# A transformer block, forward and backward, on one core: three groups of DMA issues moved in SyncE's and GpSimd's queues

## The chip, the core and the metric

The kernel runs on one core of a Trainium2 chip. The metric is the device time of one execution in microseconds (us). The time before is 819.68 us, the median of 3 runs (819.25 to 820.12).

## The reference

One layer with its gradients: S = 2048 rows, D = 640, 32 heads of 20, F = 1728, all bf16. The function returned is the layer's output and, for a given grad_out, the gradients of x, wqkv, wo, w1, w3 and w2.

```python
def _A_ref(x, wqkv, wo):                       # linear attention
    q, k, v = split_heads(x @ wqkv)
    phi = lambda t: jnp.where(t > 0, t + 1, jnp.exp(t)) + 1e-6
    pq, pk = phi(q), phi(k)
    kv = jnp.einsum("bhsd,bhse->bhde", pk, v)
    z = jnp.einsum("bhsd->bhd", pk)
    num = jnp.einsum("bhqd,bhde->bhqe", pq, kv)
    den = jnp.einsum("bhqd,bhd->bhq", pq, z)[..., None] + 1e-6
    return merge_heads(num / den) @ wo
def _B_ref(x, w1, w3, w2):                     # gated MLP
    return (jax.nn.silu(x @ w1) * (x @ w3)) @ w2
h = x + _A_ref(_layernorm(x), wqkv, wo)
h2 = h + _B_ref(_layernorm(h), w1, w3, w2)
```

(split_heads and merge_heads stand for the reference's reshapes and transposes.)

## The kernel before, in words

The rows are cut into 16 tiles of 128 (ST = 16), D into 5 blocks of 128 (DT = 5), F into 14 (FT = 14). Work is issued in the order in which the Python code runs: every engine has its own queue, executes it in order, and waits on semaphores where its data comes from another engine or from a DMA. Nothing is reordered afterwards. DMAs written `dma` and `dmaT` (a DMA that transposes) are issued by SyncE (SP), those written `dmaG` by GpSimd (POOL), some by ScalarE (ACT). A DMA issue that waits holds back all later issues of its queue.

The stages on TensorE, with the trace's times:

- 0 to 60 us: LayerNorm 1 of x, its transposed form pqT, and k for all tiles (L266 to L280). Beside it M = pk^T x is summed block by block (`m_part`, L425, L430): M's block m is a [128, 640] piece, copied out by ScalarE in `m_end` (L433, L437) and turned into mT by a DMA (L442).
- 60 to 85 us, the stretch that the change touches (L586 to L642, then the list in `run` at L950): the remaining blocks of M, q for tiles 5 to 15 (`q_tile`, `q_late`), kv = wv^T mT block by block (`kvT_block`, L444 to L451), and Wp, the product of kv and wo (`f2_wT`, L703). Each of Wp's five pieces is turned by a DMA of SyncE (L711). For each tile t, r = pq / den is made by `r_prod` (GpSimd, L367), `r_red`, `r_inv` and `r_scale` (VectorE, L374 to L381; together `r_row`), and turned into pqT by `r_T` (a DMA of SyncE, L385); `r_head` is `r_row` and `r_T`.
- 85 to 97 us: `f2_at` (L651 to L671) multiplies r's tiles 0 to 5 with Wp (L659; for some halves an identity product with x first, L657), adds x, and takes the statistics of LayerNorm 2. `f2_hn` (L750) writes the normalized tile hn. Tiles 0 and 1 are turned into hnT by a DMA of SyncE (L766 in `f2_ht`), tiles 2 and 3 by TensorE (L770) and a ScalarE copy (L771). hn is also stored to memory for the backward pass (L758).
- from 97.6 us: the MLP, four chunks of 512 rows (`mlp`, L788). Each step multiplies w1, w3 and w2^T with a chunk (`mm5_to`, L393 to L396). Then the gradients, to the end.

Loads that the change speaks of:

- `w13` (L500, L501) is a list of seven loads of w1 and w3: rows 0-255, 256-511 and 512-639 of each, and a last small one for w1's padding. `w13[4:]` is the last block of 128 rows of w1 and of w3 and the small one.
- `load_x(0, 4)` (L186) loads rows of x again into x_sb, where the normalized x was; the normalized x is what M's blocks multiply (L431).
- `load_w2T(a, b)` (L456) loads and turns rows a to b of w2.
- `f2_m_out` (L716) stores M's block 4, `r_store(5, 6)` (L735) stores r's tile 5, both from GpSimd.
- `f2_rest` (L673) finishes the held halves of tiles 4 and 5.

In `f2_hn` hn's tile 0 is not stored at once: the line reads `for n in ((), (0, 1))[t] if t < 2 else (t,)`, so that tiles 0 and 1 are stored behind the turn of tile 1.

Of the kernel before, what the change touches and what calls it, by code (L numbers as in the profile page):

```python
# [9 lines left out]
P = 128  # L10
# [13 lines left out]
W, SC, TPC = 512, 4, 4  # L24
# [31 lines left out]
def kernel(  # L56
# [20 lines left out]
    dma, dmaT, dmaG = SY.dma_start, SY.dma_start_transpose, G.dma_start  # L77

    def rows(ap):
        return ap.rearrange("(t p) d -> p t d", p=P)  # L80
# [22 lines left out]
    r_v, pk_v, xn_v, hn_v, m_v, pq_v = rows(r_d), rows(pk_d), rows(xn_d), rows(hn_d), rows(m_d), rows(pq_d)  # L103
# [82 lines left out]
    def load_x(a, b):  # L186
        dma(out=x_sb[:, a:b, :], in_=xS[:, a:b, :])
# [40 lines left out]
    def load_w13(c0, c1):  # L228
        def go1():
            dma(out=w1[:, c0:c1, 0:F], in_=rows(B_w1)[:, c0:c1, :])  # L230

        def go3(c0=c0, c1=c1):
            dma(out=w3[:, c0:c1, :], in_=rows(B_w3)[:, c0:c1, 0:F - FL])
        return [go1, go3]
# [39 lines left out]
    def p1_mm(t, n0, between=None, halves=None):  # L274
        acc = p1_acc() if halves is None else None
        for j in range(2):
            p1_half(acc[:, j, 0:HD] if halves is None else halves[j][:, 0:HD], t, n0 + j * HD)
            if j == 0 and between is not None:
                between()
        return acc  # L280
# [9 lines left out]
    def phi(acc, dst, t, parts=None):  # L290

        mq, rq = parts or phi_tiles()
        if parts is None:
            kw = dict(scale=ln1.rs[:, t:t + 1]) if t < RAW else {}
            A.activation(two(mq[:]), acc[:, :, 0:HD], AF.Exp, **kw)
            A.activation(two(rq[:]), acc[:, :, 0:HD], AF.Relu, **kw)

        def rest():
            V.tensor_scalar(out=mq[:], in0=mq[:], scalar1=1.0, scalar2=1e-6, op0=ALU.min, op1=ALU.add)
            V.tensor_tensor(out=dst, in0=mq[:], in1=rq[:], op=ALU.add)  # L300
        held.append(rest)
# [9 lines left out]
    def q_home(t):  # L311
        if t < 4 or 8 <= t < 10:
            pqs[t] = pq6[:, t if t < 4 else t - 4, :]
        elif t < 8:
            pqs[t] = pf.tile([P, D], BF16, name="pql", bufs=4)[:]
        else:
            pqs[t] = pkx[0][:, DT + t - 10, :]
# [3 lines left out]
    def q_tile(t):  # L321
        q_home(t)
        phi(p1_mm(t, 0), pqs[t], t)
# [7 lines left out]
    def z_diag(m):  # L331
        dz[m] = hx[:, 10, m * P:(m + 1) * P]
        V.tensor_scalar(out=dz[m], in0=ident[:], scalar1=Z[:, m:m + 1], scalar2=None, op0=ALU.mult)
# [25 lines left out]
    def r_prod(t):  # L359
        for j in range(2):  # L360
            js = slice(j * HD, (j + 1) * HD)
            if t < 8:
                pr[t, j] = (p1.tile([P, HD], F32, name="pr", bufs=2) if t % 2 else
                            pf.tile([P, HD], F32, name="pr", tag="h2", bufs=2))[:]
            else:
                pr[t, j] = ps.tile([P, 512], F32, name="prp", tag="at", bufs=2)[:, 0:HD]
            (G if t < 8 else V).tensor_tensor(out=pr[t, j], in0=pqs[t][:, js], in1=Zb[:, js], op=ALU.mult)  # L367
# [4 lines left out]
    def r_red(t, js=(0, 1)):  # L372
        for j in js:
            V.reduce_sum(out=rden[:, t, j * 16:(j + 1) * 16], in_=heads(pr.pop((t, j))), axis=AX.X)  # L374

    def r_inv(t):
        V.tensor_scalar(out=rden[:, t, :], in0=rden[:, t, :], scalar1=1e-6, scalar2=None, op0=ALU.add)
        V.reciprocal(out=rden[:, t, :], in_=rden[:, t, :])

    def r_scale(t):  # L380
        V.tensor_tensor(out=heads(pqs[t]), in0=heads(pqs[t]),  # L381
                        in1=rden[:, t, :].unsqueeze(2).to_broadcast([P, H, DH]), op=ALU.mult)

    def r_T(t):
        dmaT(out=pqT[:, :, t * P:(t + 1) * P], in_=pqs[t])  # L385
# [39 lines left out]
    def m_part(m, tiles, js=(0, 1)):  # L425
        if m not in macc:
            macc[m] = [ps.tile([P, 512], F32, name="macc", tag=("m", "tr")[m % 2], bufs=2) for _ in range(2)]
        for t, j in [(t, j) for t in tiles for j in js]:
            n = HD + (m < 2) * j
            T.matmul(macc[m][j][:, 0:n], lhsT=pk_all[:, t, m * P:(m + 1) * P],  # L430
                     rhs=x_ext[:, t, j * HD:j * HD + n], start=(t == 0), stop=(t == ST - 1))  # L431

    def m_end(m, js=(0, 1)):  # L433
        mb = mbs[:, m % 4, :]
        acc = macc[m]
        for j in js:
            A.copy(out=mb[:, j * HD:(j + 1) * HD], in_=acc[j][:, 0:HD])  # L437
        if m < 2:
            A.copy(out=Z[:, m:m + 1], in_=acc[1][:, HD:HD + 1])
            z_diag(m)  # L440
        if m < DT - 1:
            dmaT(out=mT[:, :, m * P:(m + 1) * P], in_=mb)  # L442

    def kvT_block(m, acc):  # L444

        a, b = M_H[m]
        n = (b - a) * DH
        for c in range(DT):
            T.matmul(acc[:, 0:n], lhsT=wqkv[:, c, 2 * D + m * P:2 * D + (m + 1) * P],
                     rhs=mT[:, c, a * DH:b * DH], start=(c == 0), stop=(c == DT - 1))  # L450
        masked(bd, acc[:, 0:n], m)  # L451
# [48 lines left out]
    w13 = [go for c0, c1 in ((0, 2), (2, 4), (4, 5)) for go in load_w13(c0, c1)]  # L500
    w13 += [lambda: dma(out=w1[:, :, F:FP], in_=rows(B_w3)[:, :, F - FL:F])]  # L501

    def load_wo():
        dma(out=wo[:], in_=A_wo.rearrange("(c p) n -> p c n", p=P))
# [69 lines left out]
    def big():  # L574
        return ps.tile([P, 2, 512], F32, name="bigx", tag="big", bufs=2)[:, 0]

    def r_row(t):
        r_red(t)
        r_inv(t)
        r_scale(t)  # L580

    def r_head(t):
        r_row(t)
        r_T(t)
# [16 lines left out]
    m_part(2, range(10, ST))  # L601
    m_end(2)
    load_wo()
    for go in w13[4:]:
        go()
    dmaG(out=m_v[:, 0, :], in_=mbs[:, 0, :])
    r_head(0)
    r_prod(2)
# [11 lines left out]
    phi_rest()  # L620
    m_part(3, range(11, ST))
    m_end(3)
    r_T(1)
    r_T(2)
    load_w2T(4 * P, 8 * P)
    dmaG(out=m_v[:, 1:4, :], in_=mbs[:, 1:4, :])
    r_head(3)
    r_prod(5)
    m_part(4, range(5))
    q_tile(8)  # L630
    kvT_block(1, big())
    r_row(4)
# [7 lines left out]
        m_part(4, range(11, ST), (j,))  # L640
        m_end(4, (j,))
    ps.release()  # L642
    load_x(0, 4)


    ps = pool("pap", space=PSUM)
    hn, hnT, hhT = {}, {}, {}
# [102 lines left out]
    def f2_hn(t):  # L750
        hn[t] = (pf.tile([P, D], BF16, name="hn", tag="pql", bufs=4) if t == 2 else
                 pf.tile([P, D], BF16, name="hn", tag="h2", bufs=2) if t == 3 else
                 pf.tile([P, D], BF16, name="hn") if t % 2 else w2[:, FT, :])
        ln2.norm(hn[t][:], x_sb[:, t, :], t)
        if t < 2:
            f2_ht(t)
        for n in ((), (0, 1))[t] if t < 2 else (t,):
            dma(out=hn_v[:, n, :], in_=hn[n][:])  # L758

    def f2_ht(t):  # L760
        c, i = divmod(t, TPC)
        if i == 0:

            hnT[c] = (U1.tile([P, DT, W], BF16, name="hnT", tag="W6") if c == SC - 1 else pqT[:, :, c * W:(c + 1) * W])
        if t >= TPC or t < 2:
            dmaT(out=hnT[c][:, :, i * P:(i + 1) * P], in_=hn[t][:])  # L766
            return
        tr = ps.tile([P, DT, P], BF16, name="trh", tag="mm", bufs=4)
        for d in range(DT):
            T.transpose(tr[:, d, :], hn[t][:, d * P:(d + 1) * P], ident[:])  # L770
        A.copy(out=hnT[c][:, :, i * P:(i + 1) * P], in_=tr[:])  # L771
# [174 lines left out]
    def kv3():  # L946
# [6 lines left out]
        (q_out, 10, 14), (mlp_ghh, 4),  # L953
        (q_late, 15), (w2_room,), (sig_table,), (f2_half, 0, 0), (f2_half, 1, 0), (f2_half, 2, 0), (f2_half, 3, 0), (mlp_ghh, 5),
        (f2_half, 0, 1), (f2_half, 1, 1), (f2_hn, 0), (f2_half, 2, 1), (f2_hn, 1),
        (f2_half, 3, 1), (f2_m_out,), (r_store, 5, 6),
        (f2_half, 4, 0, True), (mlp_ghh, 6), (f2_half, 4, 1, True), (f2_half, 5, 0, True), (r_red, 6, (0,)), (f2_hn, 2), (f2_hn, 3),
        (f2_ht, 2), (f2_ht, 3), (load_w2T, 8 * P, 10 * P), (mlp_ghh, 7), (r_red, 6, (1,)), (r_inv, 6), (r_scale, 6),
        (r_T, 6), (f2_rest,), (r_red, 7), (r_inv, 7), (r_scale, 7), (r_T, 7), (r_store, 6, 7))
    p1.release()  # L960
    pa = pool("pa", "right")

# [285 lines left out]
    for t in range(ST):  # L1248
# [14 lines left out]
        if t >= 1:  # L1263
# [3 lines left out]
            if t <= 2 * DT:  # L1267
                n = (t - 1) % DT
# [124 lines left out]
    for m, (a, b) in enumerate(M_H):  # L1393
        n = (b - a) * DH
# [84 lines left out]
    def both_grads(m, f0, f1):  # L1479

        return [(max(f0, lo) - f0, min(f1, lo + F) - f0, out[:, m, max(f0, lo) - lo:min(f1, lo + F) - lo])
                for lo, out in ((0, out4S), (F, out5S)) if max(f0, lo) < min(f1, lo + F)]
# [60 lines left out]
    for i, (f0, f1) in enumerate(blocks):  # L1543
        n = f1 - f0
        for m in range(DT):
            last = (i, m) == (len(blocks) - 1, DT - 1)
            for a, b in ((0, n - P), (n - P, n)) if last else ((0, n),):
                c = (a + b) // 2
                halves = ((a, c), (c, b)) if i * DT + m < 6 else ((a, b),)
                out = [(x + y - a, z + y - a, to) for y, w in halves for x, z, to in both_grads(m, f0 + y, f0 + w)]  # L1550
# [43 lines left out]
```

## Time and profile before

| What | Value |
|---|---|
| median of 3 runs | 819.68 us (819.25 to 820.12) |
| the profiled execution's own time | 819.31 us |
| its span in the profile | 817.4 us |
| TensorE (PE) busy | 811.9 us, 99% |
| VectorE (DVE) busy | 445.1 us, 54% |
| ScalarE (ACT) busy | 324.7 us, 40% |
| GpSimd (POOL) busy | 129.0 us, 16% |
| granted TensorE clock | 1.00 |

The span is the time from the first to the last instruction that the profile shows; the execution's own time is 1.9 us longer. The profile's page gives for each engine the time in which it executes something; the timeline gives single instructions in order, and the view of waits puts an engine's idle time down to what ended it. For a DMA there are two numbers: how long its issue took on the queue (the timeline), and how long after the start of the issue it landed (the view of DMA issues). "PEld" is TensorE's loading of the stationary operand, which runs ahead of the matmul that uses it.

### The profile page before, as it was taken

To read this page: it belongs to the slowest core of one execution; us is meant where nothing else is said; L and a number is where in the kernel's file an instruction comes from. 1 tells how busy PE (TensorE), PEld (TensorE's weight loads), DVE (VectorE), ACT (ScalarE), POOL (GpSimd) and SP (SyncE) were. 2 spreads that over 40 slices of the span, in tenths; PEclk is the share of its full clock that TensorE was granted. 3 is DMA by queue.
4 is the path that set the end of the run, shared out by engine and by line. 5 is a ranking of instruction groups with operands and counts; after the bars stand their busy time and mean duration, and the time that the engine had idled before them with its cause. 6 is when DMAs were issued, how large, how long until landed. Compare 5 with 4: busy or idle time off the path is not lost.

```text
span 817.4 us, 13576 instructions
## 1 busy us (share of the span) xinstructions
PE 811.9 (99%) x5227; PEld 494.9 (61%) x5227; DVE 445.1 (54%) x976; ACT 324.7 (40%) x607; POOL 129.0 (16%) x194
## 2 busy tenths in 40 slices
PE   8999999999999999999999999999999999999998
PEld 6777544555555555754577777777657777544444
DVE  7859997998898566300057777772565551000000
ACT  7856688665565666011122212222113442111111
POOL 2243333333222212100001111110120000000000
DMA  9899899696485556999977887259985669779981
GB/s 260 208 240 291 199 275 310 199 242 174 126 210 158 166 173 168 227 255 233 255 176 182 212 197 200 58 105 189 218 181 103 123 162 249 188 180 232 257 203 38
DMA packets 334480, 159.83 MB, mean 196 GB/s; under 512 B 252304, under 2 KB 327920, under 8 KB 334416
## 3 DMA queue, kind: packets, MB, share of 16 engines
q1 hardware_dynamic: 290976, 119.37, 63.0%
q0 software_dynamic: 7008, 23.17, 8.3%
q10 hardware_dynamic: 36432, 16.42, 8.2%
q8 instruction: 41, 0.67, 0.4%
q14 instruction: 23, 0.19, 0.1%
HBM read 44.47 MB, written 53.43 MB: 120 GB/s over the span
## 4 chain that ended last, share of the span: by engine, by line
PE 98%; DMA 1%; ACT 0%; SPq 0%; issue 0%
PE mm L395 21%; PE job L1346 20%; PE ghn L1133 14%; PE gxn L1497 8%; PE gw L1088 7%; PE big L268 4%; PE o L915 4%; PE o L861 3%; PE gwo L1221 3%; PE macc L430 3%; PE gr L1190 3%; PE dkv L1441 3%; PE at L659 3%; PE mm L268 1%; DMA wqkv<-in_A_wqkv_dram 1%; PE dkv L1380 1%
## 5 line engine op out<-in xcount | busy, mean ns | idle before, releaser
L1346 PE MATMUL job<-gb,g_q 128*128 128x496 bf16 (+3 forms) x576 | 116.8, 366 | 0.0
L1133 PEld LDWEIGHTS <-ggb 128*128 128x128 bf16 x864 | 84.5, 98 | 33.0
L395 PE MATMUL mm<-pqT,w 128*128 128x512 bf16 x405 | 93.7, 379 | 0.2 <-DMA pqT<-hn 0.2
L1346 PEld LDWEIGHTS <-g_q 128*128 128x128 bf16 x576 | 55.8, 98 | 61.0
L395 PEld LDWEIGHTS <-w 128*128 128x128 bf16 x540 | 52.5, 98 | 63.3 <-DMA pqT<-hn 0.6
L1350 ACT CAST obs<-job 128x496 bf16<-128x496 f32 (+4 forms) x56 | 28.6, 511 | 134.3 <-PE job L1346 128.7
L1133 PE MATMUL ghn<-w13a,ggb 128*128 128x320 bf16 x448 | 63.5, 299 | 0.0
L1133 PE MATMUL ghn<-w13b,ggb 128*128 128x320 bf16 x416 | 61.4, 299 | 0.0
L1148 DVE SCALAR_TENSOR_TENSOR wb<-gs,hnb 128x640 f32<-128x640 bf16 x16 | 13.2, 826 | 88.1 <-ACT gs L1145 88.1
L395 PE MATMUL mm<-g2T,w2T 128*128 128x512 bf16 x240 | 59.6, 379 | 0.0
L1088 PE MATMUL gw<-hb,g 128*128 128x512 bf16 (+2 forms) x320 | 58.6, 346 | 0.0
L1088 PEld LDWEIGHTS <-g 128*128 128x128 bf16 x320 | 31.3, 98 | 26.9
L420 ACT CAST ghh<-mm 128x512 bf16<-128x512 f32 x48 | 28.1, 585 | 47.8 <-PE mm L395 41.7
L1198 POOL TENSOR_TENSOR sz<-Zb,g_h 128x640 f32<-128x640 bf16 x16 | 20.2, 1261 | 163.9 <-DVE g_h L1199 163.9
L798 ACT ACTIVATE sig<-mm 128x512 bf16<-128x512 f32 x56 | 33.7, 602 | 25.7 <-PE mm L395 21.7
L1145 ACT ACTIVATE gs<-ghn 128x640 bf16<-128x640 f32 x16 | 11.2, 703 | 75.4 <-PE ghn L1133 75.4
L395 PEld LDWEIGHTS <-w2T 128*128 128x128 bf16 x260 | 25.4, 98 | 23.4
L268 PEld LDWEIGHTS <-pqT 128*128 128x128 bf16 x320 | 30.7, 98 | 14.0 <-issue 1.3
L1346 PEld LDWEIGHTS <-g 128*128 128x128 bf16 x320 | 31.0, 98 | 12.8
L268 PE MATMUL big<-wqkv,pqT 128*128 128x320 bf16 x250 | 38.4, 299 | 0.2
L834 DVE TENSOR_TENSOR gate<-gate,sig 128x1024 bf16<-128x1024 bf16 x28 | 19.3, 690 | 33.8 <-ACT gate L809 31.0
L1093 ACT CAST gw2o<-gw 128x512 bf16<-128x512 f32 (+2 forms) x20 | 10.4, 519 | 67.2 <-PE gw L1088 24.7
(213 smaller groups left out, 1378.3 us busy)
## 6 DMA issues: line engine op xcount, KB each, us to landing
hh_d<-hhT SPq DMA_DIRECT2D x24, 256.0 KB, 2.7
gg_d<-gate POOLq DMA_DIRECT2D x24, 256.0 KB, 3.8
gg_d<-ghh POOLq DMA_DIRECT2D x24, 256.0 KB, 4.3
ggb<-gg_d SPq DMA_DIRECT2D x6, 896.0 KB, 5.4
ggb<-gg_d ACTq DMA_DIRECT2D x6, 832.0 KB, 5.4
ggb<-gg_d SPq DMA_DIRECT2D x2, 1728.0 KB, 12.7
x_sb<-in_A_x_dram SPq DMA_DIRECT2D x4, 640.0 KB, 4.9
pk_d<-pk_all SPq DMA_DIRECT2D x4, 640.0 KB, 5.5
```

Of the source, the lines that this page charges most:

```text
L268: T.matmul(acc, lhsT=pqT[:, c, t * P:(t + 1) * P], rhs=wqkv[:, c, n0:n0 + HD], start=(c == 0), stop=(c == DT - 1))
L395: T.matmul(acc[:], lhsT=w[:, c, fc * P:(fc + 1) * P], rhs=rhs[:, c, :], start=(c == 0), stop=(c == DT - 1))
L420: A.copy(out=ghh[n // 2][:, n % 2, :], in_=acc[:])
L430: T.matmul(macc[m][j][:, 0:n], lhsT=pk_all[:, t, m * P:(m + 1) * P], rhs=x_ext[:, t, j * HD:j * HD + n], start=(t == 0), stop=(t == ST - 1))
L659: T.matmul(at[:, 0:HD], lhsT=pqT[:, c, t * P:(t + 1) * P], rhs=Wp[:, c, j * HD:(j + 1) * HD], start=(c == 0 and not on_pe), stop=(c == DT ...
L798: A.activation(sig[:, i, :], gp[:], AF.Sigmoid)
L915: T.matmul(o2["ps"][:, 0:HD], lhsT=hhT[c][:, fc, i * P:(i + 1) * P], rhs=w2[:, fc, j * HD:(j + 1) * HD], start=(fc == 0), stop=(fc == FT - 1))
L1088: T.matmul(acc[:, 0:fw], lhsT=g2[:, t, m * P:(m + 1) * P], rhs=hb[b][:, t, 0:fw], start=(t == 0), stop=(t == ST - 1))
L1133: T.matmul(acc[:, j, 0:HD], lhsT=ggb[t // 2][:, k, lo:lo + P], rhs=rhs[:, j * HD:(j + 1) * HD], start=(k == 0), stop=(k == NG - 1))
L1346: T.matmul(acc[:, 0:n], lhsT=lhs[:, t, m * P:(m + 1) * P], rhs=rhs(t), start=(t == 0), stop=(t == ST - 1))
L1350: A.copy(out=ob, in_=acc[:, 0:n])
L1497: T.matmul(acc[:, j, 0:HD], lhsT=g, rhs=wqT[:, k, j * HD:(j + 1) * HD], start=(k == 0), stop=(k == 14))
```

## The change

Three groups of issues move; the arithmetic and the order of the compute instructions stay.

1. The three loads of `w13[4:]` were issued behind the load of wo; they are now issued behind `m_end(3)`, that is, behind the turn of M's block 3 (the fourth), and behind the turn of r's tile 0, which lay after them.
2. `load_x(0, 4)` was issued behind M's block 4; it is now issued behind the first five tiles of that block, ahead of the turn of r's tile 3. For this the turn `r_T(3)` is taken out of `r_head(3)`.
3. Six stores of 160 KB each move: hn's tiles 0 to 3 (SyncE) from `f2_hn` to a new function `hn_out` behind the load of rows 1024 to 1279 of w2; M's block 4 and r's tile 5 (GpSimd) to behind `f2_rest`.

```diff
     m_end(2)
     load_wo()
-    for go in w13[4:]:
-        go()
     dmaG(out=m_v[:, 0, :], in_=mbs[:, 0, :])
     r_head(0)
...
     m_part(3, range(11, ST))
     m_end(3)
+    for go in w13[4:]:
+        go()
     r_T(1)
     r_T(2)
     load_w2T(4 * P, 8 * P)
     dmaG(out=m_v[:, 1:4, :], in_=mbs[:, 1:4, :])
-    r_head(3)
+    r_row(3)
     r_prod(5)
     m_part(4, range(5))
+    load_x(0, 4)
+    r_T(3)
     q_tile(8)
...
     ps.release()
-    load_x(0, 4)
...
         if t < 2:
             f2_ht(t)
-        for n in ((), (0, 1))[t] if t < 2 else (t,):
-            dma(out=hn_v[:, n, :], in_=hn[n][:])
+        if t >= TPC:
+            dma(out=hn_v[:, t, :], in_=hn[t][:])
+
+    def hn_out():
+        for t in range(TPC):
+            dma(out=hn_v[:, t, :], in_=hn[t][:])
...
-        (f2_half, 3, 1), (f2_m_out,), (r_store, 5, 6),
+        (f2_half, 3, 1),
         (f2_half, 4, 0, True), (mlp_ghh, 6), (f2_half, 4, 1, True), (f2_half, 5, 0, True), (r_red, 6, (0,)), (f2_hn, 2), (f2_hn, 3),
-        (f2_ht, 2), (f2_ht, 3), (load_w2T, 8 * P, 10 * P), (mlp_ghh, 7), (r_red, 6, (1,)), (r_inv, 6), (r_scale, 6),
-        (r_T, 6), (f2_rest,), (r_red, 7), (r_inv, 7), (r_scale, 7), (r_T, 7), (r_store, 6, 7))
+        (f2_ht, 2), (f2_ht, 3), (load_w2T, 8 * P, 10 * P), (hn_out,), (mlp_ghh, 7), (r_red, 6, (1,)), (r_inv, 6), (r_scale, 6),
+        (r_T, 6), (f2_rest,), (f2_m_out,), (r_store, 5, 6), (r_red, 7), (r_inv, 7), (r_scale, 7), (r_T, 7), (r_store, 6, 7))
```

## The prediction

> **What bounds the kernel now.** I read the page's busy rows first, then TensorE's own waits, then the chain of waits around the change, and last SyncE's timeline, because the change reorders DMA issues and nothing else. The engines' instruction order, compared for the two kernels, is the same on TensorE, VectorE and ScalarE; SyncE's and GpSimd's issues move.
>
> ```profile
> PE 811.9 (99%) x5227; PEld 494.9 (61%) x5227; DVE 445.1 (54%) x976; ACT 324.7 (40%) x607; POOL 129.0 (16%) x194
> PE   8999999999999999999999999999999999999998
> ```
>
> TensorE is busy in 811.9 of 817.4 us, and the two slices below 9 are the first and the last. Of the 5.5 us that are left, the windows of 20 us put 2.6 in the first 20 us, 2.7 behind the last matmul, and 0.2 between 80 and 100. All the rest is 20.00 of 20.00. So at most a few tenths can be won anywhere the change reaches, and anything that makes TensorE wait is paid in full. TensorE's waits name the one stall:
>
> ```profile
> PE warm L468 <- DVE zero L125: 1.1, 1, 1.1
> PE k L268 <- DMA wqkv<-in_A_wqkv_dram: 1.1, 2, 0.6
> PE tr L258 <- ACT x_sb L479: 0.2, 1, 0.2
> PE mm L395 <- DMA pqT<-hn: 0.2, 1, 0.2
> ```
>
> The first three are at the start, before the change. The fourth is tile 1 of hn, turned by DMA (L766), for which the first product of the MLP waits. The chain from 60 to 110 us shows it (start, us, what); everything else there is TensorE back to back:
>
> ```profile
> 94.14 0.18 PE at L659 x2
> 94.32 3.28 DMA pqT<-hn
> 97.60 0.04 issue
> 97.64 8.81 PE mm L395 x40
> ```
>
> SyncE's timeline (start, us of the issue) is the queue into which the change cuts:
>
> ```profile
> 60.41 0.61 SPq L504 DMA_DIRECT2D wo<-in_A_wo_dram  x1
> 61.07 1.41 SPq L230 DMA_DIRECT2D w<-in_B_w_dram  x1
> 62.52 0.45 SPq L233 DMA_DIRECT2D w<-in_B_w_dram  x1
> 63.01 0.47 SPq L501 DMA_DIRECT2D w<-in_B_w_dram  x1
> 63.59 4.17 SPq L385 DMA_TRANSPOSE pqT<-hx  x1
> 67.85 2.46 SPq L442 DMA_TRANSPOSE mT<-hx  x1
> 70.42 2.54 SPq L385 DMA_TRANSPOSE pqT<-hx  x2
> 73.01 2.81 SPq L457 DMA_TRANSPOSE w2T<-in_B_w_dram  x1
> 75.93 1.26 SPq L385 DMA_TRANSPOSE pqT<-hx  x1
> 77.28 1.45 SPq L187 DMA_DIRECT2D x_sb<-in_A_x_dram  x1
> 79.64 6.51 SPq L711 DMA_TRANSPOSE Wp<-pkx  x5
> ```
>
> **Part 1, the three weight loads** (432, 416 and 80 KB; the 61.07, 62.52 and 63.01 rows) go behind the turn of M's block 3. The view of DMA issues, asked in narrow windows, gives issue to landing: 9.1, 8.7 and 8.5 us, so they land by 71.5; block 3 (67.85) takes 7.1 and lands at 74.95, and its first reader, the kv product L449, starts at 75.36. In the new order r's tile 0 can issue at 61.07 (its data was ready at 60.01) and block 3 as soon as ScalarE has copied it (L437 ends at 66.43), not at 67.85; it queues behind wo, which lands at 69.0, and should land near 71. TensorE did not wait for it before, so these 4 us win nothing. The weights are then issued at about 67.8 to 70.2 and land by 79 even at their old 9 us. Their first reader starts at 97.64, so they cost nothing; the cover is 18 us.
>
> **Part 2, x rows 0 to 3 ahead of the turn of r's tile 3.** The load overwrites rows that M's block 4 reads; those five pairs of products are the last of the L430 x20 that begin at 64.42 and last 2.72, so it waits for nothing. The turn's landing, 4.3 us behind 75.93, is 80.2 now; behind x it is some 2 us later, and its reader, the fourth group of L659 (85.17 + 3 x 0.68 = 87.2), has 5 us in hand. x itself lands at 82.4 and is added at 86.3. Cost nothing.
>
> What both parts do share is **SyncE's arrival at Wp**. The first Wp turn issues at 79.64, when its data is there; SyncE had been free since 78.73. From there the five leave 1.31 us apart, and the third (82.26, 2.7 us to landing) lands at 84.93; TensorE's first weight load for L659 starts at 85.03. That is 0.1 us of margin. SyncE's new order, with the rows' own times: block 3 from 66.5, 1.26; weights 2.33; two turns 2.54; w2T 2.81; x 1.45; turn 1.26; with the gaps it is done at about 78.5. So 1.1 us of cover is left ahead of 79.64 and I take no cost. The upper bound is the 4.17 and 2.46 us rows: turns whose issue stretched while wo and the three weights were in front and had not landed. If the two turns behind the weights take these instead of 1.27 each, SyncE is 4.1 us later, 3.0 past 79.64, and TensorE stands 2.9 us. I take the lower end because when the turn of tile 1 comes up, near 70.2, wo has landed; in front are block 3 and the weights, about what was in front at 70.4 in this trace, where the two turns took 2.54.
>
> **Part 3, six stores.** hn's four stores (L758: 0.57 + 1.93 of SyncE, 95.58 to 98.13) go behind the w2T load (1.33, at 98.19), and m's last block and r's tile 5 (GpSimd, 95.19 and 95.77, 160 KB each) behind the rest of tiles 4 and 5. Until now the turn of hn tile 1 took 3.3 us to land, with those two GpSimd stores and the first hn store issued 0.9 to 1.5 us into it; the turn of tile 0 took 2.6 with none, and the five Wp turns 2.6 to 3.4, median 2.7. At 2.65 the turn lands at 96.97. TensorE's five matmuls before the wait start at 96.24 and follow each other at 0.216 (1.08 for five in the chain), so the next could go at 97.32; it went at 97.64. **The gain is 0.32 us.** Bounds: 0 if the turn takes 3.3 again; at most 0.32, because the next thing due is ScalarE's copy of tiles 2 and 3 (95.95 + 1.29 = 97.24), then TensorE itself. The w2T load now follows the turn directly, but tile 0's turn had tile 1's directly behind it and took 2.6, so I do not count a loss.
>
> The Trainium skill, "DMA: Bandwidth & Descriptors", section "Queues, rings and completion order", says that a DMA's semaphore write lands only after every earlier write of that DMA engine, in whichever queue. By it stores of GpSimd's queue that move in front of the last bytes hold the turn's semaphore, and the sum is the full 0.32; the 3.3 against 2.6 fits, though this trace alone does not prove the cause.
>
> What the moved stores could hold up: hn's reach memory by about 102, and the buffer of tile 0 is written again at 105.93 (L161); SyncE's next turn, r's tile 6, keeps its place near 99.5, because the sum of issues is the same. GpSimd issues 1.1 us more after 100.64, ends near 103.0, and its next work starts at 107.58. r's tile 5 must land before its buffer is reloaded at 111.57. w2T comes earlier. All cost nothing; behind 100 us TensorE has no idle time in this trace, and a start 0.3 us earlier moves the rest with it.
>
> **Sum.** 819.31 (profiled execution: span 817.4 plus 1.9 around it) - 0.32 = 819.0. The median of the runs shown is 819.68, 0.37 above the profiled one, so on that scale the forecast is **819.4 us**.
>
> **Rivals.**
> The gap stays (0.18): the load of w2T, 256 rows turned, takes the stores' place on the DMA engines right behind the turn, and something else made it slow. For it: one of the five Wp turns took 3.4 with no GpSimd store issued in its time. Against: that one had x in front of it, and tile 0 took 2.6. It gives 819.7. The Trainium skill, same page, section "Issuing engines are not separate DMA queues", speaks for this: all queues run on the same 16 DMA engines, so moving work between or along queues frees no bandwidth.
>
> SyncE late at Wp (0.12): the mechanism above, at L711. It decides once more than 1.2 us of issue time is added ahead of 79.64, and from there each further us is one of TensorE. If the first turn behind the weights takes 4.17 instead of 1.22, SyncE is 1.8 past 79.64, TensorE waits 1.7, and 819.68 + 1.7 - 0.3 = **821.1**; with both long rows 822.3. For it: 0.1 us margin at the third Wp turn. Against: wo out of the way.
>
> The change does not do what it says: the instruction lists show the moves, so this has no chance of its own. Something not seen here: 0.04, mostly (0.03) a gain over what the one stall allows.
>
> **How the numbers follow.** Forecast 0.66, gap stays 0.18, late Wp 0.12, unseen 0.04. The forecast's own range is 819.0 to 819.8. Reaching over the gap case (819.7, with the runs' 0.4 on either side 820.1) and the smaller of the late cases, the range is 818.8 to 820.6. A difference under 0.2% (1.64 us) is about what a measurement of this kernel can tell from no change. Both main cases lie inside it; of the late case half is beyond. Faster 0.03, same 0.90, slower 0.07.
>
> **What would show it.** Right: the wait of L395 for pqT<-hn gone, the turn landing in about 2.7 us, TensorE at 20.00 in every 20 us but the first and last, mT's block 3 landing before 72, the first Wp turn still issuing at 79.6. Wrong: a wait of L659 for Wp<-pkx near 85 us, the turns behind the weights taking 3 to 4 us to issue, or the L395 wait still there. A time below 818 would mean that the traced execution hides stalls that others have.

## The result and the profile after

| | before | changed |
|---|---|---|
| median, 22 runs each | 819.64 us | 821.1 us |
| lowest to highest | 819.08 to 820.7 | 818.89 to 822.97 |
| profiled execution, its span | 819.31, 817.4 | 820.43, 818.5 |

The ratio is 1.0017, 95% interval 1.001 to 1.0023: the changed kernel is 1.4 us slower. Its runs also spread over 4.1 us, those of before over 1.6, and its best run is faster than any of before.

TensorE's waits in the changed kernel (us in total, times, longest):

```profile
PE at L660 <- DMA Wp<-pkx: 1.3, 2, 0.9
PE warm L468 <- DVE zero L125: 1.1, 1, 1.1
```

The wait of L395 for hn's turn is gone, as forecast. In its place TensorE waits twice for Wp, 0.86 and 0.45 us. SyncE's timeline (start, us of the issue) shows where that begins:

```profile
60.21 0.60 SPq L504 DMA_DIRECT2D wo<-in_A_wo_dram  x1
60.91 4.60 SPq L385 DMA_TRANSPOSE pqT<-hx  x1
66.27 1.20 SPq L442 DMA_TRANSPOSE mT<-hx  x1
67.52 0.57 SPq L230 DMA_DIRECT2D w<-in_B_w_dram  x1
68.14 0.42 SPq L233 DMA_DIRECT2D w<-in_B_w_dram  x1
68.61 0.43 SPq L501 DMA_DIRECT2D w<-in_B_w_dram  x1
69.16 5.01 SPq L385 DMA_TRANSPOSE pqT<-hx  x2
74.22 2.82 SPq L457 DMA_TRANSPOSE w2T<-in_B_w_dram  x1
77.13 0.53 SPq L187 DMA_DIRECT2D x_sb<-in_A_x_dram  x1
77.76 1.21 SPq L385 DMA_TRANSPOSE pqT<-hx  x1
79.45 7.52 SPq L712 DMA_TRANSPOSE Wp<-pkx  x5
```

SyncE reaches Wp in time: 79.45, and it had been free since 78.97. But the five Wp turns now take 7.52 us to issue, not 6.51; the third leaves at 83.08 instead of 82.26. And the DMA engines are behind. w2T, issued 1.2 us later, lands 7.2 us behind its issue instead of 6.4, at 81.4 instead of 79.4, although SyncE's queue has the same bytes in front of it. (The 6.4 of before is itself long: in the traces of five kernels below, which keep the large weight loads behind wo or hand them over early, w2T lands 4.9 to 5.2 us behind its issue, at 77.6 to 77.9.) The loss of throughput stands in the windows of 2 us (the last two columns are the DMA engines' busy share and GB/s), first before, then changed:

```profile
68.00:70.00 2.00, 2.00 (x20) 1.50 (x19) 1.90 (x5) 1.30 (x2) 0.89 (x2) 1.00 1.05 389
70.00:72.00 2.00, 2.00 (x17) 1.46 (x15) 1.90 (x5) 0.17 (x1) 1.53 (x2) 1.00 1.21 298
```

```profile
68.00:70.00 2.00, 2.00 (x20) 1.53 (x18) 1.90 (x5) 1.30 (x2) 0.76 (x2) 1.00 1.23 211
70.00:72.00 2.00, 2.00 (x17) 1.43 (x16) 1.90 (x4) 0.36 (x1) 1.48 (x2) 1.00 0.98 256
```

Just where the weights were moved to, the DMA engines carry 934 KB in 4 us instead of 1374. The first weight load lands 4.5 us behind its issue, at 72.0, and block 3's turn ahead of it at 66.27 + 3.5 = 69.8: 2.2 us between two landings, where the same 432 KB took 1.1 behind wo (69.0 to 70.2).

The second wait, from the chain (start, us, what):

```profile
85.75 4.75 DMA Wp<-pkx
90.50 0.05 issue
90.55 0.85 PE at L660 x5
```

The fifth Wp turn takes 4.75 us to land, in the kernel before 2.6. It left 0.3 us behind GpSimd's 640 KB store of q (L731, issued at 85.44, landing 4.3 us later); in the kernel before it left 0.7 us ahead of that store.

From 60 us to the first MLP product the changed kernel needs 1.3 us more: 98.77 against 97.64, with a start of wo's issue that was 0.2 earlier.

### The profile page after: what moved, and what is told of

It reads as the page before. It is cut to its first block, busy times and chain, and to the rows that moved or that the text cites. A ratio compares the mean times of both kernels' runs of the same rounds, so it can differ in the third digit from the quotient of the medians.

```text
span 818.5 us, 13574 instructions
## 1 busy us (share of the span) xinstructions
PE 813.0 (99%) x5227; PEld 495.7 (61%) x5227; DVE 445.2 (54%) x976; ACT 324.3 (40%) x607; POOL 129.1 (16%) x194
## 4 chain that ended last, share of the span: by engine, by line
PE 98%; ACT 1%; DMA 1%; issue 0%; DVE 0%; ACTq 0%
PE mm L395 20%; PE job L1351 20%; PE ghn L1138 14%; PE gxn L1502 8%; PE gw L1093 7%; PE big L268 4%; PE o L920 4%; PE o L866 3%; PE gwo L1226 3%; PE macc L430 3%; PE gr L1195 3%; PE dkv L1446 3%; PE at L660 2%; PE mm L268 1%; PE dkv L1385 1%; DMA Wp<-pkx 1%
## 5 line engine op out<-in xcount | busy, mean ns | idle before, releaser
L395 PE MATMUL mm<-pqT,w 128*128 128x512 bf16 x405 | 93.6, 379 | 0.0
L395 PEld LDWEIGHTS <-w 128*128 128x128 bf16 x540 | 52.6, 98 | 62.9 <-issue 0.6
L395 PE MATMUL mm<-g2T,w2T 128*128 128x512 bf16 x240 | 59.6, 379 | 0.0
L1150 ACT ACTIVATE gs<-ghn 128x640 bf16<-128x640 f32 x16 | 11.2, 703 | 77.6 <-PE ghn L1138 77.6
L395 PEld LDWEIGHTS <-w2T 128*128 128x128 bf16 x260 | 25.4, 98 | 23.4
```

The lines of the kernel that those rows point to most:

```text
L395: T.matmul(acc[:], lhsT=w[:, c, fc * P:(fc + 1) * P], rhs=rhs[:, c, :], start=(c == 0), stop=(c == DT - 1))
```

## The experiments

Each kernel was timed beside the kernel before on the same chip, and each ratio is against the median of before that belongs to it: 819.46 for the first four; 819.53 for the small load moved, the group of copies, the weights with x and q's store behind f2's halves; 820.16 for the other four.

**The three parts one by one.** Part 1 alone, part 2 alone, part 3 alone, and parts 2 and 3 without part 1; the edits are those of the diff above.

> The kernel before with part 1 alone: the three weight loads behind the turn of M's block 3. Theory S (the DMA engines stand for about a microsecond each time SyncE's queue goes from a turning DMA to a copy or back; part 1 puts the weights between turns and so adds two such switches): slower by 1.0 to 2.0 us, w2T's 512 rows land near 81 instead of 79.4, the third Wp turn lands after 85.3, TensorE waits for Wp. Rival X (x ahead of r's tile 3 is the cause, part 2): no difference, within 0.3 us. My prediction's own sum: 0.

> The kernel before with part 2 alone: x rows 0 to 3 ahead of the turn of r's tile 3. Theory S: the number of switches between turns and copies is the same, so within 0.4 us of before; the switch back to turns falls nearer to Wp, so a small loss is possible. Rival X: slower by 1.0 us or more, third Wp turn late.

> The kernel before with part 3 alone: the six stores moved. Prediction's term: faster by 0.32 us, the turn of hn's tile 1 lands in about 2.65 us instead of 3.3 and TensorE's wait for it is gone. Rival (gap stays): no difference, the turn still takes 3.3.

> The changed kernel without part 1. Theory S: the loss is gone; faster than before by 0.3 us (part 3's term), at most 0.4 slower; no wait for Wp over 0.2 us. Rival X: slower by 1 us, as the changed kernel.

| kernel | median | ratio, 95% interval |
|---|---|---|
| part 1 alone | 820.71 | 1.0014 (1.0005 to 1.0022) |
| part 2 alone | 819.78 | 1.0 (0.9991 to 1.0009) |
| part 3 alone | 819.12 | 0.9999 (0.9991 to 1.0008) |
| parts 2 and 3 | 819.17 | 0.9999 (0.9989 to 1.001) |

Part 1 carries the whole loss, and rival X falls. (The profiled execution of part 1 was the slowest of its runs, 822.06; it has the same two waits, 1.4 us, and it is late ahead of the change too: wo issues at 61.75, 1.3 us later than in the kernel before.) Part 3 does in the trace what the prediction said; the turn of hn's tile 1 lands 2.6 us behind its issue, and TensorE's list of waits has only the start left:

```profile
PE warm L468 <- DVE zero L125: 1.1, 1, 1.1
PE k L268 <- DMA wqkv<-in_A_wqkv_dram: 0.2, 1, 0.2
```

Its medians differ by 0.34 us, the size forecast, but the interval does not tell that from nothing.

**Why part 1 leaves a hole: switches, bytes, or time of issue.** The hole is the stretch at 68 to 72 us in which the DMA engines carry less. The expectations set three theories against each other. S: each switch of SyncE's queue between turns and copies costs the engines about a microsecond. It was formed on the packets at 69 to 72 us, some of which took over 1 us where the queue goes from turns to copies. B: what costs is the bytes brought closer to Wp. E: the weights are handed over too late to follow on. Six kernels try them. In the first only the 80 KB load is moved:

```diff
-    for go in w13[4:]:
+    for go in w13[4:6]:
         go()
...
     m_end(3)
+    w13[6]()
```

> The kernel before with only the smallest of the three loads (80 KB, w1's padding) behind the turn of M's block 3; the two large loads stay behind wo. Theory S (switches between turns and copies cost, not bytes): as part 1 alone, 0.7 to 1.5 us slower than before, packets that hang for over 1 us where the small load begins and w2T's landing 1.5 us later against wo's issue. Rival B (it is the bytes in front of the turns): within 0.3 us of before.

819.89, ratio 1.0002 (0.9993 to 1.0011); the small load lands 0.4 us behind block 3's turn, and w2T 5.0 us behind its issue. The small load had 4.3 us of work in front of it at its issue; there the switch cost little.

Weights and x in one group of copies, two switches fewer than in the changed kernel:

```diff
     m_end(3)
-    for go in w13[4:]:
-        go()
-    r_T(1)
-    r_T(2)
-    load_w2T(4 * P, 8 * P)
...
     m_part(4, range(5))
+    for go in w13[4:]:
+        go()
     load_x(0, 4)
+    r_T(1)
+    r_T(2)
+    load_w2T(4 * P, 8 * P)
     r_T(3)
```

> The changed kernel with the weights and x rows 0 to 3 issued as one group of copies behind the turn of M's block 3, ahead of r's tiles 1 and 2, w2T, r's tile 3 and Wp. The same loads as in the changed kernel, two switches fewer, none close to Wp. Theory S: the loss is gone, 0.3 us faster than before (part 3's term), within 0.4 us of it at worst. Rival B (late weights by their place and bytes): 1 us slower or more, as the changed kernel.

821.53, ratio 1.0025 (1.0016 to 1.0034): slower, against S. The first weight load again takes 2.1 us behind block 3's turn. SyncE itself comes to Wp 2 us late (81.65), since the issue of w2T takes 4.94 us here, and the turns land behind the q store: 5.3 us for the fourth. TensorE waits 1.2, 0.4 and 0.3 us there; the view puts the 1.2 down to VectorE, but it ends at 87.05, 0.1 us behind the landing of the third Wp turn. Since a late SyncE is a cause of its own, this kernel alone does not decide between S and E.

The weights right ahead of x, behind r's tile 3:

> The changed kernel with the three weight loads still later, directly ahead of x and behind r's tile 3, so that the number of switches is that of the kernel before. Theory S: no wait for Wp over 0.3 us, within 0.4 us of before. Rival B (930 KB brought closer to Wp): slower than the changed kernel, 2 us or more over before, Wp's first turn landing 2 us later.

819.79, ratio 1.0004 (0.9995 to 1.0013). No loss that can be told from nothing, with one wait of 0.4 us for Wp: rival B's 2 us are refuted. S foretold this one, and so the switch was still in question after it.

More switches than in the changed kernel (a turn between the weight loads), and the small load first:

```diff
     m_end(3)
-    for go in w13[4:]:
-        go()
+    w13[4]()
     r_T(1)
+    w13[5]()
+    w13[6]()
     r_T(2)
```

> The changed kernel with the turn of r's tile 1 put between the first weight load and the other two: one more turn, copy, turn change. Theory S: each return from a turn to a large load costs about 1.2 us, so the second load takes 2.1 instead of 1.56 and w2T lands 1 us later than in the changed kernel; 1 us slower than it. Rival E: within 0.4 us of the changed kernel.

> The changed kernel with the smallest of the three loads first. Theory S: the small load takes the pause at the switch, the large ones then 1.1 us each, the total unchanged: as the changed kernel, 821.1. Rival E: the same total too, but the pause stays with the first large load. Time within 0.5 us of the changed kernel by both; the landings tell them apart.

819.5, ratio 0.9995 (0.9987 to 1.0004), and 820.02, ratio 1.0002 (0.9992 to 1.0012). Neither is slower than before, so S's price for a further switch is refuted; and both are faster than either theory expected. With the small load first the pause was shared: that load took 1.7 us behind the turn. And in this kernel's windows the engines carry still less than in the changed kernel, 846 KB, yet TensorE has no wait for Wp:

```profile
68.00:70.00 2.00, 2.00 (x20) 1.50 (x19) 1.90 (x5) 1.30 (x2) 0.88 (x2) 1.00 1.06 216
70.00:72.00 2.00, 2.00 (x17) 1.45 (x15) 1.90 (x5) 0.19 (x1) 1.53 (x2) 1.00 0.81 207
```

So a hole alone costs TensorE nothing; it costs where it leaves the engines too far behind at Wp (the table of backlogs below).

Now the weights between the turns of r's tile 0 and of block 3, so that SyncE need not wait for block 3 before it hands them over:

```diff
     r_head(0)
+    for go in w13[4:]:
+        go()
...
     m_end(3)
-    for go in w13[4:]:
-        go()
```

> The changed kernel with the three weight loads one place earlier, between the turns of r's tile 0 and of M's block 3. They still go from a turn to copies and back, as in the changed kernel, but SyncE hands them over some 2 us sooner, while wo is still landing. Theory S (the switch itself costs): the first weight load takes 2.1 us or more of the DMA engines between landings (1.1 in the kernel before), w2T lands 2 us later than before, slower than before by 1 us. Rival E (in the changed kernel the queue runs nearly dry while block 3 waits for ScalarE, and the weights come too late to fill it): the first weight load takes 1.1 to 1.4, w2T lands within 0.6 us of before, and the kernel is 0.3 us faster than before.

819.09, ratio 0.999 (0.9981 to 0.9998): faster than before, though the interval only just says so, and the lowest ratio of all the kernels. The order is still turn, copies, turn. SyncE's timeline and the windows:

```profile
61.09 4.39 SPq L385 DMA_TRANSPOSE pqT<-hx  x1
65.53 0.57 SPq L230 DMA_DIRECT2D w<-in_B_w_dram  x1
66.15 0.42 SPq L233 DMA_DIRECT2D w<-in_B_w_dram  x1
66.62 0.43 SPq L501 DMA_DIRECT2D w<-in_B_w_dram  x1
67.15 1.55 SPq L442 DMA_TRANSPOSE mT<-hx  x1
...
79.67 6.51 SPq L712 DMA_TRANSPOSE Wp<-pkx  x5
```

```profile
68.00:70.00 2.00, 2.00 (x19) 1.52 (x18) 1.90 (x5) 1.30 (x2) 0.92 (x2) 1.00 1.15 320
70.00:72.00 2.00, 2.00 (x17) 1.45 (x15) 1.90 (x5) 0.15 (x1) 1.53 (x2) 1.00 1.15 325
```

Issued 2.0 us sooner, the first load lands at 70.5, 1.1 us behind the turn ahead of it (61.09 + 8.3 = 69.4), as in the kernel before. At its issue that turn had 3.9 us left to land; in the changed kernel block 3's turn had 2.3. The windows carry 1290 KB again, and Wp issues in 6.51. So the hole is rival E's: SyncE waits for block 3, and the weights come too late to follow on.

The packets in the traces show what the hole is made of. In the changed kernel the first packets of the 432 KB load start 1.7 us behind its issue; the first 16 of its 128 take 0.77 us in the median, 23 take over 0.3 and the longest 1.5, while the later ones take 0.135. Where the load is issued behind wo or behind r's tile 0, no packet takes over 0.3. So the engines do not stand idle in the hole, and their busy share hardly drops: they hold the load's first packets for long.

**The fifth Wp turn and q's store.** The store is moved, in the changed kernel, behind f2's second halves of tiles 0 and 1, and in another kernel behind r's tile 5:

```diff
-        (q_out, 10, 14), (mlp_ghh, 4),
+        (mlp_ghh, 4),
...
-        (f2_half, 0, 1), (f2_half, 1, 1), (f2_hn, 0), (f2_half, 2, 1), (f2_hn, 1),
+        (f2_half, 0, 1), (f2_half, 1, 1), (q_out, 10, 14), (f2_hn, 0), (f2_half, 2, 1), (f2_hn, 1),
```

> The changed kernel with one store moved: the 640 KB store of q's tiles 10 to 13 (GpSimd, L731), which issued between the fourth and the fifth Wp turn, goes behind the second halves of tiles 0 and 1 (f2_half). If the fifth Wp turn is late because that store is in front of it: it lands 2.6 us behind its issue instead of 4.75, the second wait of L660 (0.45 us in the changed kernel's trace) is gone and the kernel is 0.4 us faster than the changed one; the first wait (0.86) stays. Rival (the fifth turn is only late because SyncE is late): no difference.

> The changed kernel with the 640 KB store of q's tiles 10 to 13 behind both critical groups of turns, after r's tile 5. If that store in front of the fifth Wp turn (0.45 us in the changed kernel's trace), and in front of hn's turns in the kernel that had it there (1.3), is what makes them late: no wait for the fifth Wp turn and none for hn, so 0.3 to 0.6 us faster than the changed kernel, about 820.5. Rival: no difference from the changed kernel, 821.1.

822.16, ratio 1.003 (1.002 to 1.004), and 828.35, ratio 1.01 (1.0086 to 1.0114). In both the fifth Wp turn lands 2.6 us behind its issue and its wait is gone, as expected. What was expected of the times is wrong in both, because the store hits something else. In the first it issues at 94.45, between the issues of hn's two turns, and these land in 3.5 and 4.8 us:

```profile
PE mm L395 <- DMA pqT<-hn: 1.3, 1, 1.3
```

This 1.3 us takes the place of the changed kernel's 1.3. The traced execution is still 1.7 us longer than that of the changed kernel (822.14 against 820.43), and 1.6 of it lie ahead of wo's issue (61.77 against 60.21), which no edit reaches; whether that holds for the other runs of this kernel is not known.

In the second it lands at 107.3 (103.37 + 3.9), and ScalarE's first sigmoid of the MLP starts at 107.54, after 7.46 us without work:

```profile
PE mm L395 <- ACT up L810: 5.9, 1, 5.9
PE at L660 <- DMA Wp<-pkx: 0.9, 1, 0.9
```

In the trace the sigmoid's wait names the semaphore of this store; it lasts 8.1 us and ends as the store lands. The sigmoid's output lies in pool pa, allocated where p1 is released (L965, L966 there), and the store reads pkx of p1.

## Why the prediction was off, point by point

- **What bounds the kernel** held: TensorE pays for every wait in full.
- **Part 3, 0.32 us gained**: right in mechanism, and 0.34 by the medians of part 3 alone; the 3.3 us of hn's turn became 2.6 in each kernel with the stores out of the way, but for the one that put q's store there. That the w2T load now follows directly did not slow the turn, so "the gap stays" fell. In part 1 alone, with the stores not moved, the turn took 2.6 too: there the first of them issued 1.2 us into it, not 0.8 to 1.0 as in the three traces where it took 3.2 to 3.4. So the gain seems to hang on a few tenths of a microsecond.
- **Part 2, nothing**: 819.78 against 819.46, not to be told apart.
- **Part 1, nothing**: this is the step that failed, in its sentence on SyncE's new order, "I take no cost". The rows that I added up were SyncE's issue times, and their sum came out (78.5 forecast, 78.97 measured), but by luck: the two turns behind the weights took 5.01 us to issue, not the 2.54 of the lower end that I chose, and the weights and x took 1.8 us less than their old rows (1.42 and 0.53, not 2.33 and 1.45). What I left out was the time of the DMA engines themselves. I took their backlog as given, the bytes being the same. But the new order makes SyncE stand from 65.5 to 66.3 for block 3, with only two turns of 0.5 us and the rest of wo in front of the engines, and the next load came too late to follow on. At the first Wp issue the engines were 4.4 us behind, not 2.7, the third Wp turn landed at 85.75 instead of 84.93, and TensorE waited 0.86 us for it; the fifth turn added 0.45.
- **Late Wp, 821.1 us, 0.12**: the rival that came, but by another route, so that its time was met is luck. SyncE was on time; the first two Wp issues took 1.41 and 2.02 us, not 1.2, while the engines were behind, and the fifth turn fell behind q's store, which I had not looked at. The price of a long issue ahead of Wp (1.7) was not what happened.
- **The range** ended at 820.6 because only the smaller late cases were let in. The 0.1 us margin of the third Wp turn, which I had seen, should have made this rival heavier.

How the wait goes with the backlog can be read across the kernels. The first column is the landing of the last DMA ahead of Wp minus the first Wp issue, the second TensorE's wait for Wp in that trace, in us:

| kernel | backlog at Wp | wait |
|---|---|---|
| parts 2 and 3; part 2; small load moved | 2.0; 2.4; 2.5 | 0 |
| weights behind r's tile 0; before | 2.6; 2.7 | 0 |
| split weights; part 3 | 3.1; 3.2 | 0 |
| small load first; q's store behind f2's halves | 3.5; 3.5 | 0 |
| part 1 | 3.8 | 1.4 |
| weights with x | 3.9 | 0.4 |
| changed; q's store at the end | 4.4; 4.5 | 1.3; 0.9 |

(The kernel with one group of copies stands apart, since SyncE came 2 us late.) Up to 3.5 us nothing happens; from 3.8, the next value measured, TensorE waits. Of the 1.3 and 1.4 us of the changed kernel and of part 1, 0.45 and 0.5 belong to the fifth turn and q's store, so what goes with the backlog is 0.9. The changed kernel is not far above this edge, which would fit its wide spread; that its shorter executions have less backlog was not traced. Part of the spread lies ahead of the change: in these traces wo issues anywhere between 60.2 and 61.8 us.

On the fifth turn the Trainium skill helps. "DMA: Bandwidth & Descriptors", section "Queues, rings and completion order", says that each DMA engine takes turns between the queues, and that a semaphore write lands only after all earlier writes of that engine, in whichever queue. By the first alone, I reckon that a 160 KB turn beside a 640 KB store should lose about its own transfer time; by the second it waits for whatever of the store is in front. The traces fit the second better: 4.7 us instead of 2.6, landing 0.7 us behind the store (89.8, then 90.5). No run separates the two.

What stays open: why the first packets of a load that is handed over late take so long. In seven traces with such a load (all kernels with the weights behind block 3 but the one with the small load first) it lands 4.2 to 4.7 us behind its issue, whether 1.4 or 2.4 us of work was in front. That looks like a time which the load needs by itself, with the 2.2 us between landings as what the work in front did not cover; but no run issues it with nothing in front, and none tells reading from memory from other causes.

## What to carry to other kernels

A DMA moved behind a producer that its queue has to wait for can reach the DMA engines too late to follow on, and the microsecond lost can return at the next transfer that has no margin; so the engines' backlog, landing by landing, belongs in the sum next to the issue times. A turn whose landing sets the end needs the other queues' large stores behind it, not ahead of it. And before a store is moved to a later place, see who is waiting for the memory it reads.

## What the runs showed of the hardware that was not expected

- A 640 KB store from GpSimd, issued between 1.3 us ahead of the issue of a SyncE turn of [128, 640] and 0.6 us behind it, took the turn's landing from 2.6 us to between 3.3 and 5.3 (seven turns of Wp and hn in five kernels). Issued 0.7 us behind it, as in the kernel before, it left the 2.6.
- The issue of such a turn, 1.20 us at best, stretched to 1.4 and 2.0 while the engines were 4.4 us behind, and to 4.6 right behind the 800 KB load of wo; the w2T issue, 2.8, stretched to 4.94.
- 432 KB took 1.1 us between landings when 3.9 us of work or more was in front of the load at its issue, and 1.9 to 3.3 when it was 1.4 to 2.4 (seven kernels; the two add up to 4.2 to 4.7).
